# A fused adaLN transformer block: the last four quads in token halves, spaced modulation pieces, and three banks for VectorE's tiles

## The chip, the cores and the metric

The kernel runs on one core of a Trainium2 chip. The metric is device time in microseconds of one execution. Before the change the median of 3 runs is 764.55 us (762.23 to 765.07). The engines are TensorE (PE, matmuls into PSUM), VectorE (DVE), ScalarE (ACT), GpSimd (POOL) and SyncE (SP, which issues nearly all DMAs). PSUM has 8 banks of 512 fp32 columns.

## The reference

One block with adaptive layer norm: six modulation vectors come from `c`, attention with 32 heads of 16 columns follows, then a feed-forward of 1376 columns; S = 2048 tokens, D = 512, bf16 inputs.

```python
mod = (silu(c) @ w_mod).reshape(1, 6, 1, -1)
sa, ca, ga, sb, cb, gb = (mod[:, i] for i in range(6))
h = layernorm(x) * (1 + ca) + sa
x = x + ga * attention(h, wqkv, wo)         # softmax(q k^T / 4) v, 32 heads
h = layernorm(x) * (1 + cb) + sb
x = x + gb * (gelu(h @ w1 + b1) @ w2 + b2)
```

## The kernel before

**Work.** The tokens form four blocks b of 512. A quad is one block of queries with four heads, one in each 32-row strip of PE; there are 32 quads, in order of block. A quad has 16 key tiles for each of its four heads, so there are 32 x 64 = 2048 score tiles of 128 keys by 512 queries. A score tile is one matmul (`qk`, L819). Then it is exponentiated in one of two ways. ScalarE takes two or three PSUM banks at once with an exact exp into `PB` (L1254). VectorE takes one bank (`TB`, L1349): it makes the bits of a power of two as an int16, shifts the result twice (L1383), and PE adds the three approximations with the scaled values `VV`. The products with the values (L1028) add up in PSUM bank 7, the only one for this, so one quad's sum must be copied out (`emit_out`, L1304, into `o_sb`, a ring of two buffers) before the next may start.

**Normalizing a quad.** The softmax denominators lie in rows of `o_sb`. SP carries them through DRAM into `dall`, VectorE inverts them (L1319), SP carries them back, spread over rows, into `RB[par]` (L1324), and POOL multiplies (L1328) and adds the even and odd quads of a pair into `OT` (L1331). The last two quads are split instead into two halves of 256 tokens each (`LAST = NQ - 2`, `emit_half`): shuffle, reciprocal and product on VectorE (L1285 to L1289), with no trip through DRAM. Key tiles are paired there, so that a score tile again has 512 columns.

**Banks.** Exp groups of ScalarE use the zones (0, 1) and (3, 4); zone (0, 1) takes bank 2 as a third when it is free (`EXTRA`). VectorE's tiles use banks 6 and 5 (`D_BANKS`). All other matmuls, "sums" such as projections and feed-forward, take a free one of 2, 5 and 6 (`BG_BANKS`).

**Order.** The program writes every engine's instructions out by hand order at build time: a loop keeps a clock for each engine, and `step_pe`, `step_act`, `step_dve` and `run_alone` choose what that engine does next by planned durations. A step has `needs` (labels) and a `pos`: it may start when so many score tiles have been issued. `D_LOAD` and `D_ALONE` bound how much planned VectorE work may be waiting when another tile is given to VectorE. Fillers (L1092, L1095) are matmuls on zeros that PE does when too little has streamed in the last 3.4 us.

**Around attention.** `mod2_pieces` makes the second modulation's columns with 32 matmuls of one column (L496), in eight pieces. `tail_steps(b, base, sp)` holds, for blocks 0 to 2, the output projection, residual, norm and feed-forward, at positions spread by `SPREAD[b]`; its bias is added by VectorE (L604) and one GELU per block runs on ScalarE over 5632 columns (L614), which costs a table load there and another back. `last_steps` does the same for block 3 in two halves (`half(0)`, `half(1)`): the output projection's sum is added to `x1` (L673), `bn_stats` (L189) reads `x1`, POOL takes the root, then norm (L692), transposes (L699), up-projection (L708), GELU straight from PSUM on ScalarE (L712, only when no exps are left), down-projection (L720), residual and output (L727, L728).

Of the kernel before, what the change touches and what calls it, by code (L numbers as in the profile page):

```python
# [11 lines left out]
ALU = mybir.AluOpType  # L12
# [32 lines left out]
KEEP = 0.72  # L45
NQM = 5
# [3 lines left out]
D_BANKS = (6, 5)  # L50
BG_BANKS = (2, 5, 6)
BG_STRICT = False
D_LOAD = 2300.0
D_ALONE = 1400.0
# [16 lines left out]
SPREAD = (1.0, 1.0, 1.0)  # L71
# [16 lines left out]
def adaln_block(ctx: ExitStack, tc: tile.TileContext, A_x, A_wqkv, A_wo, B_x, B_w1, B_b1, B_w2, B_b2,  # L88
# [274 lines left out]
    LAST = NQ - 2  # L363
    quads += quads[LAST:]
    QN = NQ + 2
# [8 lines left out]
    class Step:  # L374
        def __init__(self, kind, eng, dur, fn, needs=(), label=None, pos=0, pieces=(), dt=FP32, alt=None, pdur=226.0,
                     mark=None):
            self.kind, self.eng, self.dur, self.fn = kind, eng, dur, fn
            self.needs, self.label, self.pos = tuple(needs), label, pos
            self.pieces, self.dt, self.alt, self.pdur = list(pieces), dt, alt, pdur
            self.bank, self.ready, self.done = None, None, 0  # L380
            self.only, self.gate, self.mode = False, None, "f" if dt is BF16 or label == "mod2" else "p"
# [123 lines left out]
    mm(mod2_pieces(), mod2_evac, 250.0, "mod2", [], rows_at, FP32, None, 260.0)  # L505
# [132 lines left out]
    def last_steps(base):  # L638
# [18 lines left out]
        op("SP", 0.0, begin, ("tb", b), [("te", b - 1)], base - 100)  # L657
        op("SP", 0.0, lambda: None, "spare", [], base - 60)

        def half(hf):  # L660
            tts = (2 * hf, 2 * hf + 1)
            cs = slice(256 * hf, 256 * hf + 256)
            at = base + 52 * hf

            def o_pieces(tt):
                def one(i, key, ch):
                    def f(ps):
                        mm4(ps, OT[key][:, tt * P:(tt + 1) * P], W_o[:, ch, :], i == 0, i == NC)
                    return f
                return [one(i, key, ch) for i, (key, ch) in enumerate(parts)]  # L670

            def o_evac(tt):
                return lambda ps, e: nc.vector.tensor_tensor(out=T["x1"][:, tt, :], in0=ps, in1=T["x1"][:, tt, :],  # L673
                                                             op=ALU.add)

            for tt in tts:
                x = mm(o_pieces(tt), o_evac(tt), 600.0, ("o", b, tt),
                       [("ot", b, ch) for ch in range(NC - 1)] + [("last", hf, 0), ("tb", b), ("wo", NC - 1)], at)
                x.gate = (NC, [("last", hf, 1)])
                op("DVE", 600.0, lambda tt=tt: ln_stats(T["x1"], T["st"], tt, tt), ("s2", b, tt), [("o", b, tt)])  # L680
# [8 lines left out]
            op("POOL", ROOT_L, root, ("r2", hf, b), [("a2", hf, b)])  # L689
            for i, tt in enumerate(tts):  # L690
# [3 lines left out]
                op("DVE", 325.0, norm, ("n2", hf, i), [("r2", hf, b), "spare"])  # L694
# [11 lines left out]
            for fc in range(NFC):  # L706
# [4 lines left out]
                def up(ps, e, fc=fc):  # L711
                    nc.scalar.activation(out=T["u"][:, fc, cs], in_=ps[:, 0:256], func=ACT.Gelu_apprx_tanh,  # L712
                                         bias=late["b1c"][:, fc:fc + 1], scale=1.0)
                x = mm([one(j) for j in range(NC)], up, 380.0, ("u3", hf, fc), [("h3", hf, j) for j in range(NC)],
                       at + 6, FP32, 380.0, 108.0)
                x.only, x.mode = True, "f"
# [14 lines left out]
            for tt in tts:  # L731
                x = mm(d_pieces(tt), d_evac(tt), 600.0, ("d", b, tt),
                       [("u3", hf, fc) for fc in range(NFC)] + [("w2", NFC - 1)], 2046 + hf, FP32, None,
                       216.0)
# [69 lines left out]
    def tok_of(qi):  # L804
        if qi < LAST:
            return slice(0, 512)
        hf = (qi - LAST) // 2
# [85 lines left out]
    def due_sum(t):  # L893
# [4 lines left out]
        for s in sums:  # L898
            if s.pos > scored[0]:
                return None  # L900
            if s.bank is None:
# [7 lines left out]
    def pe_burst(t, z):  # L909
        bs = list(ZONES[z]) if z is not None else []  # L910
        x = EXTRA[z] if z is not None else None
        if x is not None and free[x] <= t and not (busy_sum[0] is None and reserve(t)):
# [17 lines left out]
        if d_wanted(t):  # L930
            for r in d_rows(used):
# [3 lines left out]
                b_ = next((i for i in D_BANKS if free[i] <= t and i not in [x[0] for x in dp]), None)  # L935
# [102 lines left out]

    def pe_sum(t):
        s = busy_sum[0]  # L1040
        if s is None:
# [3 lines left out]
            if s.bank is None:  # L1045
                b_ = bg_bank(t)
                if b_ is None:
                    return False
                s.bank = b_
                free[b_] = INF  # L1050
            else:
# [8 lines left out]
        if s.gate and s.done == s.gate[0] and not has(s.gate[1], clk["PE"]):  # L1060
            sums.remove(s)
            held.append(s)
            busy_sum[0] = None
# [45 lines left out]
    def step_pe_work(t):  # L1109
# [32 lines left out]
        have = busy_sum[0] is not None or (due_sum(t) is not None and bg_bank(t) is not None)  # L1142
# [3 lines left out]
        if have:  # L1146
            s = busy_sum[0] or due_sum(t)
# [15 lines left out]
    def pool_ok(s, t):  # L1163
# [6 lines left out]
        if s.label[0] == "vv" or t > s.ready + POOL_WAIT:  # L1170
# [5 lines left out]
    def run_alone(e, t, maxpos=None):  # L1176
        n = 0
        for s in alone:
            if s.eng != e:
                continue  # L1180
            if s.pos <= scored[0] and has(s.needs, t):
                if e == "POOL" and not pool_ok(s, t):
# [3 lines left out]
                alone.remove(s)  # L1186
                made = s.fn()
                if e == "POOL" and made is not None:
# [9 lines left out]
                if e == "POOL" and s.label != "late" and s.label[0] not in ("r", "r2"):  # L1198
                    plock[0] = clk[e]
                if s.label is not None:  # L1200
# [22 lines left out]
    def take_evac(e, t):  # L1223
        for s in evacs:
            if s.only and (e == "DVE" or any(rowq) or filled):
                continue
            if s.ready + (0.0 if e == "DVE" else L_PA - L_PE) <= t and (e == "DVE" or s.alt is not None):
# [4 lines left out]
                free[s.bank] = v  # L1232
# [4 lines left out]
    def step_act(t):  # L1237
# [29 lines left out]
        if not warm and not any(rowq) and not filled:  # L1267
# [9 lines left out]
    warm = []  # L1277

    def emit_half(qi, t):
        hf, par = divmod(qi - LAST, 2)  # L1280
# [4 lines left out]
        nc.vector.tensor_copy(out=o[:, cs], in_=PS[:, 7, cs])  # L1285
        od_free[0] = t + 334.0 + L_DVE
        nc.vector.stream_shuffle(out=rs[:, cs], in_=o[:, cs], mask=[16 - par] * 32)
        nc.vector.reciprocal(out=rs[:, cs], in_=rs[:, cs])
        nc.vector.scalar_tensor_tensor(out=OT["last", par][:, cs], in0=o[:, cs], scalar=pmask[:, par:par + 1],  # L1289
                                       in1=rs[:, cs], op0=ALU.mult, op1=ALU.mult)  # L1290
        clk["DVE"] = t + 2950.0
# [279 lines left out]
```

## Time and profile before

| | us |
|---|---|
| median of 3 runs | 764.55 |
| the profiled execution | 765.63 |
| its span, first to last instruction | 763.9 |
| ScalarE: exps (L1254) busy | 679.3 |
| VectorE: tile fills (L1349) and shifts (L1383) busy | 368.3 and 221.9 |
| block 2's last output eviction (L626) starts | 723.1 |
| block 3's x is loaded (L652 issued) | 724.2 |
| last exp ends | 734.1 |
| first and last GELU of block 3 (L712) start | 738.2 and 751.7 |

All times of rows are from the span's start. The page lists busy time by engine and by line; the views by stretch, of waits and of the timeline cut the same execution in other ways. A row's mean is the duration of one instruction, and consecutive instructions of an engine overlap a little, so the distance between starts is shorter. The granted clock is the share of full speed that PE had.

### The profile page before, as it was taken

Reading aid. Unit: us, or ns where it says so; the run is one execution under the profiler, and the core shown is the slowest. Engines: PE = TensorE matmul, PEld = TensorE weight load, DVE = VectorE, ACT = ScalarE, POOL = GpSimd, SP = SyncE. Lnnn points to the kernel's source line nnn. Section 1 sums busy time; section 2 is a strip of 40 time slices with the busy share of each in tenths; the row PEclk is TensorE's granted clock in tenths of the full one; section 3 lists DMA queues with packets and bytes.
Section 4 is the critical chain, followed back from the end, with each engine's and each line's share of the span. In section 5 each row is a group of like instructions: output and inputs, shape, how many; then the busy total and the mean of one; then the engine's idle time right before and its main releaser. Section 6 shows DMA issues by size and latency. Waiting matters only on the chain.

```text
span 763.9 us, 20459 instructions
## 1 busy us (share of the span) xinstructions
PE 737.2 (97%) x8478; PEld 258.7 (34%) x8478; DVE 700.5 (92%) x1450; ACT 721.7 (94%) x671; POOL 108.9 (14%) x134
## 2 busy tenths in 40 slices
PE   3999999999999999999999999999999999999997
PEld 2433233233333333332333333332333332333454
DVE  6859999699999999988999999999899999999982
ACT  2889999899999999999999999999999999999982
POOL 3460010214232010100001110100101110100110
PEclk9999999799999999999999999999999999999999
DMA  8300000041010000000010000000000000000000
GB/s 274 112 2 11 10 6 6 9 151 16 10 37 9 10 4 8 9 16 24 15 38 3 15 4 10 9 17 12 22 18 30 9 10 9 9 10 23 21 28 31
DMA packets 27572, 20.43 MB, mean 27 GB/s; under 512 B 13801, under 2 KB 23386, under 8 KB 27474
## 3 DMA queue, kind: packets, MB, share of 16 engines
q1 hardware_dynamic: 26946, 19.07, 9.0%
q8 instruction: 68, 1.11, 0.6%
q14 instruction: 30, 0.25, 0.1%
q10 hardware_dynamic: 528, 0.00, 0.0%
HBM read 16.45 MB, written 2.61 MB: 25 GB/s over the span
## 4 chain that ended last, share of the span: by engine, by line
PE 57%; ACT 26%; DVE 9%; issue 5%; DMA 2%; SPq 1%; POOL 0%; ACTq 0%; DVEq 0%
ACT PB L1254 23%; PE PS L819 20%; PE PS L1028 18%; PE PS L406 12%; DVE TB L1349 4%; DVE TB L1383 2%; ACT uG L614 2%; PE PS L1092 2%; DMA xb<-in_A_x_dram 1%; PE PS L720 1%; PE PS L708 1%; PE PS L1095 1%; PE PS L213 1%; DVE st L189 1%; ACT L1254 0%
## 5 line engine op out<-in xcount | busy, mean ns | idle before, releaser
L1254 ACT ACTIVATE PB<-PS 128x1024 bf16<-128x1024 f32 x623 | 679.3, 1299 | 9.5 <-PE PS L819 7.7
L1349 DVE TENSOR_SCALAR TB<-PS 128x512 int16<-128x512 f32 x556 | 368.3, 682 | 22.1 <-PE PS L819 20.6
L819 PE MATMUL PS<-qm,kT 32*128 32x512 bf16 (+1 forms) x2176 | 301.9, 372 | 5.8 <-ACT PB L1254 2.8
L1028 PE MATMUL PS<-PB,VE 128*32 128x512 bf16 (+1 forms) x1589 | 252.0, 374 | 0.3 <-ACT PB L1254 0.3
L1383 DVE TENSOR_SCALAR TB<-TB 128x1024 int16<-128x1024 int16 x556 | 221.9, 421 | 5.3 <-PE PS L1028 0.5
L1028 PE MATMUL PS<-TB,VV 128*32 128x512 f16 (+1 forms) x1174 | 219.8, 374 | 0.3 <-DVE TB L1383 0.2
L819 PEld LDWEIGHTS <-kT 32*128 32x128 bf16 x2176 | 81.1, 91 | 244.5 <-issue 236.0
L1028 PE MATMUL PS<-TB,VE 128*32 128x512 f16 (+1 forms) x587 | 148.4, 375 | 1.2 <-DVE o_sb L1304 1.2
L1028 PEld LDWEIGHTS <-VE 128*32 128x32 bf16 x2176 | 69.0, 94 | 82.2 <-issue 72.1
L1028 PEld LDWEIGHTS <-VV 128*32 128x32 bf16 x1174 | 55.0, 95 | 43.7 <-issue 38.7
L1092 PE MATMUL PS<-W_q,zero 128*32 128x256 bf16 x360 | 66.7, 273 | 1.8 <-DVE TB L1349 1.4
L1328 POOL TENSOR_TENSOR OT<-o_sb,rb 128x512 bf16<-128x512 f32 x15 | 19.1, 1274 | 252.4 <-DVE TB L1383 140.7
L1328 POOL TENSOR_TENSOR o_sb<-o_sb,rb 128x512 f32<-128x512 f32 x15 | 19.1, 1270 | 247.4 <-DVE TB L1383 199.2
L406 PE MATMUL PS<-W,uG 128*32 128x512 bf16 x528 | 44.8, 383 | 0.0
L406 PE MATMUL PS<-h2T,W 128*32 128x512 bf16 x528 | 43.4, 384 | 0.2 <-DVE TB L1349 0.2
L1092 PEld LDWEIGHTS <-zero 128*32 128x32 bf16 x360 | 33.0, 96 | 23.2 <-issue 8.4
L1095 PE MATMUL PS<-W_q,zero 128*32 128x256 bf16 x163 | 34.4, 276 | 0.0
L604 DVE TENSOR_SCALAR uG<-PS,b1c 128x512 bf16<-128x512 f32 x33 | 24.6, 744 | 0.2
L406 PE MATMUL PS<-W_o,OT 128*32 128x512 bf16 x272 | 21.0, 383 | 0.6 <-DVE OT L1289 0.6
L1304 DVE COPY o_sb<-PS 128x512 f32<-128x512 f32 x30 | 20.4, 680 | 0.0
L1331 POOL TENSOR_TENSOR OT<-OT,o_sb 128x512 bf16<-128x512 bf16 x15 | 17.4, 1162 | 20.8 <-DVE TB L1383 11.7
L406 PE MATMUL PS<-hT,W_q 128*32 128x512 bf16 x240 | 20.0, 384 | 0.2 <-DVE TB L1349 0.2
(110 smaller groups left out, 401.6 us busy)
## 6 DMA issues: line engine op xcount, KB each, us to landing
rb<-d SPq DMA_DIRECT2D x120, 32.0 KB
W_m<-in_w_mod_dram SPq DMA_DIRECT2D x3, 1024.0 KB
xr<-in_A_x_dram SPq DMA_DIRECT2D x4, 512.0 KB
out_dram<-ob SPq DMA_DIRECT2D x16, 128.0 KB
xb<-in_A_x_dram SPq DMA_DIRECT2D x3, 512.0 KB
W<-in_B_w_dram SPq DMA_DIRECT2D x1, 1376.0 KB
W<-in_B_w_dram SPq DMA_DIRECT2D x1, 1280.0 KB
xb<-in_A_x_dram SPq DMA_DIRECT2D x4, 128.0 KB
```

The lines of the kernel that those rows point to most:

```text
L406: nc.tensor.matmul(out=ps[cols, :], lhsT=lhsT[:, cols], rhs=rhs, start=start, stop=stop)
L604: return lambda ps, e: nc.vector.tensor_scalar(out=T["u"][:, fc, :], in0=ps, scalar1=late["b1c"][:, fc:fc + 1], scalar2=None, op0=ALU.add)
L819: nc.tensor.matmul(out=bk(bank)[:, seg(qi, i)], lhsT=kT[32 * r:32 * r + 32, ch, kt[i] * P:(kt[i] + 1) * P], rhs=qm[(b, ch)][32 * r:32 * r ...
L1028: nc.tensor.matmul(out=PS[32 * r:32 * r + 32, 7, tok_of(qi)], lhsT=wt, rhs=src[:, seg(qi, i)], start=not started[qi][r], stop=todo[qi][r] ...
L1092: nc.tensor.matmul(out=PS[0:32, b_, 0:256], lhsT=zero, rhs=W_q[:, 0, 0:256], start=True, stop=True)
L1095: nc.tensor.matmul(out=PS[32 * o_:32 * o_ + 32, 7, c_:c_ + 256], lhsT=zero, rhs=W_q[:, 0, 0:256], start=False, stop=False)
L1254: nc.scalar.activation(out=PB[:, at:at + n, :], in_=PS[:, b0:b0 + n, :], func=ACT.Exp, bias=-KEXP * math.log(2.0), scale=math.log(2.0) / STEP)
L1304: made = nc.vector.tensor_copy(out=o, in_=bk(7))
L1328: return nc.gpsimd.tensor_tensor(out=o if par else ot, in0=o, in1=rb, op=ALU.mult)
L1331: return nc.gpsimd.tensor_tensor(out=ot, in0=ot, in1=o, op=ALU.add)
L1349: made = nc.vector.tensor_scalar(out=TB[:, u["a"]["s"], i:i + n, :], in0=PS[:, b0:b0 + n, :], scalar1=T_BIAS, scalar2=0.0, op0=ALU.add, op ...
L1383: made = nc.vector.tensor_scalar(out=TB[:, s, 0:n, :], in0=TB[:, a["s"], 0:n, :], scalar1=float(MJ[j] - MJ[j - 1]), scalar2=None, op0=ALU.add)
```

## The change

Four things change, with the planned costs that go with them.

- **Halves.** `HV = 4`: the last four quads, not two, run in token halves, in the order 28 to 31 for tokens 0 to 255 and then 28 to 31 for tokens 256 to 511. Quads 28 and 29 keep the normalization through DRAM and POOL, in halves; 30 and 31 use `emit_half`. The last half-quad of all skips its copy out of PSUM. The first half's projection, norm and up-projection come among the last exps: VectorE adds the bias, and one GELU per half runs when the exps are over (`gelu_raw`). The residual is now added on PE, with the identity times `x1` as the first piece of the sum; `bn_stats` reads PSUM, and `x1` is copied out of PSUM after the statistics. A down-projection of the last half starts before its last three GELUs.
- **Modulation.** After each of its eight pieces the step rests 1500 ns of planned time (`rest`), keeping its bank.
- **Banks.** VectorE's tiles use banks 5, 6 and 2; ScalarE's third bank is taken only if more than one of them is free (`X_FREE`). Both load bounds are lower.
- **Block 2's tail** is spread over 0.65 of the distance.

```diff
+HV = 4
+MOD_REST = 1500.0
-D_BANKS = (6, 5)
+D_BANKS = (5, 6, 2)
-D_LOAD = 2300.0
+D_LOAD = 1800.0
+X_FREE = 1
-D_ALONE = 1400.0
+D_ALONE = 900.0
-SPREAD = (1.0, 1.0, 1.0)
+SPREAD = (1.0, 1.0, 0.65)
...
-    LAST = NQ - 2
+    LAST = NQ - HV
     quads += quads[LAST:]
-    QN = NQ + 2
+    QN = NQ + HV
...
-    mm(mod2_pieces(), mod2_evac, 250.0, "mod2", [], rows_at, FP32, None, 260.0)
+    mm(mod2_pieces(), mod2_evac, 250.0, "mod2", [], rows_at, FP32, None, 300.0).rest = MOD_REST
...
-        op("SP", 0.0, begin, ("tb", b), [("te", b - 1)], base - 100)
-        op("SP", 0.0, lambda: None, "spare", [], base - 60)
+        op("SP", 0.0, begin, ("tb", b), [("te", b - 1)], 1880)
+        op("SP", 0.0, lambda: None, "spare", [], 1920)
...
-            at = base + 52 * hf
+            early = HV == 4 and hf == 0
+            raw = []
+            at = base + 52 * hf if HV == 2 else (1950, 2032)[hf]
...
-                return [one(i, key, ch) for i, (key, ch) in enumerate(parts)]
+                return [lambda ps: mm4(ps, ident, T["x1"][:, tt, :], True, False)] + [
+                    one(i, key, ch) for i, (key, ch) in enumerate(parts)]
...
+                    nc.vector.bn_stats(out=T["st"][:, tt, :], in_=ps)
...
+                    nc.vector.tensor_copy(out=T["x1"][:, tt, :], in_=banks[tt])
...
+                    if e == "dve":
+                        raw.append(fc)
+                        nc.vector.tensor_scalar(out=T["u"][:, fc, cs], in0=ps[:, 0:256],
+                                                scalar1=late["b1c"][:, fc:fc + 1], scalar2=None, op0=ALU.add)
+                    else:
+                        nc.scalar.activation(out=T["u"][:, fc, cs], in_=ps[:, 0:256], func=ACT.Gelu_apprx_tanh,
+                                             bias=late["b1c"][:, fc:fc + 1], scale=1.0)
-                x.only, x.mode = True, "f"
+                x.only, x.mode = "late" if early else True, "f"
+
+            def gelu_raw():
...
+                    u = T["u"][:, 0:len(raw), cs]
+                    nc.scalar.activation(out=u, in_=u, func=ACT.Gelu_apprx_tanh)
...
+                       ([("g3", hf)] if early else []) + [("u3", hf, fc) for fc in range(NFC - 3)] + [("w2", NFC - 1)],
+                       2046 + hf, FP32, None, 216.0)
+                x.gate = (NFC - 3, [("u3", hf, fc) for fc in range(NFC - 3, NFC)])
...
-        if x is not None and free[x] <= t and not (busy_sum[0] is None and reserve(t)):
+        if (x is not None and free[x] <= t and not (busy_sum[0] is None and reserve(t))
+                and sum(1 for i in D_BANKS if free[i] <= t) > X_FREE):
             bs.append(x)
...
+        if s.rest and s.done < len(s.pieces):
+            s.ready = clk["PE"] + s.rest
             busy_sum[0] = None
             return True
...
+            if s.label[0] == "d" and s.pos >= 2046 and ("n2", 1, 1) not in rdy:
+                continue
...
     def emit_half(qi, t):
+        src = PS[:, 7, cs] if qi == QN - 1 else o[:, cs]
+        if qi < QN - 1:
+            nc.vector.tensor_copy(out=src, in_=PS[:, 7, cs])
...
     def emit_out(qi, t):
+        hf = None if qi < LAST else (qi - LAST) // HV
+        if hf is not None and (qi - LAST) % HV >= HV - 2:
             return emit_half(qi, t)
...
+        cs = tok_of(qi)
+        n = cs.stop - cs.start
...
+        made = nc.vector.tensor_copy(out=o[:, cs], in_=PS[:, 7, cs])
...
+                nc.sync.dma_start(out=rb[rows, cs], in_=d2[r:r + 1, :].to_broadcast([16, n]))
...
+            return nc.gpsimd.tensor_tensor(out=(o if par else ot)[:, cs], in0=o[:, cs], in1=rb[:, cs], op=ALU.mult)
```

Also new: while scores are over, a down-projection may be set aside for a step of an earlier position (`paused`); POOL's products no longer wait for cover in the last three half-quads; the separate warm-up activation of GELU (L1269) is dropped.

More of the change, by code (lines that the diff above doesn't have):

```diff
@@ L900, in due_sum @@
                 return None
+            if s.rest and s.bank is not None and s.done < len(s.pieces) and t >= s.ready:
+                return s
             if s.bank is None:
@@ L934, in pe_burst @@
                     continue
-                b_ = next((i for i in D_BANKS if free[i] <= t and i not in [x[0] for x in dp]), None)
+                b_ = next((i for i in D_BANKS if free[i] <= t and i not in bs[:len(take)] + [x[0] for x in dp]), None)
                 if b_ is None:
@@ L1199, in run_alone @@
                     plock[0] = clk[e]
+                if s.frees is not None:
+                    free[s.frees.bank] = clk[e] + L_DVE
                 if s.label is not None:
```

136 lines of the change are left out of this document (86 added, 50 removed).

## The prediction

> **What bounds the kernel now.** I read the page's busy shares first, then busy time by stretches of 16 to 20 us, then the exp groups by shape, the waits, and the last 30 us as a timeline.
>
> ```profile
> span 763.9 us, 20459 instructions
> PE 737.2 (97%) x8478; PEld 258.7 (34%) x8478; DVE 700.5 (92%) x1450; ACT 721.7 (94%) x671; POOL 108.9 (14%) x134
> ```
>
> PE's 97% is the weakest of these: it is pipelined, and its row holds 523 filler matmuls (L1092, L1095), work that nothing needs. ScalarE and VectorE bind: they share the 2048 score tiles, and from 160 to 734 us both are busy in nearly every stretch. So I price the middle in tiles. Exp groups by shape:
>
> ```profile
> L1254 ACT ACTIVATE PB<-PS 128x1024 bf16<-128x1024 f32 x365 | 387.6, 1136 | 1.7 <-PE PS L819 1.2 <-PE PS L1028 0.2
> L1254 ACT ACTIVATE PB<-PS 128x1536 bf16<-128x1536 f32 x240 | 373.4, 1556 | 5.6 <-PE PS L819 4.3 <-PE PS L1028 1.2
> ```
>
> From one exp's start to the next the trace has 0.904 us after two banks and 1.331 after three: 0.452 and 0.444 us a tile. VectorE's tile costs 0.60 (a fill, L1349, start to next start) and 0.33 (its share of the shifts, L1383): 0.93. Together 2.25 + 1.08 = 3.33 tiles per us, so 1 us of VectorE work is worth 0.32 us of span and 1 us of ScalarE work 0.68. Two places fall short of that rate. The first, by stretches (PE, weight loads, DVE, ACT, POOL; granted clock after them):
>
> ```profile
> 136.00:152.00 16.00, 15.75 (x149) 4.35 (x148) 9.10 (x19) 13.34 (x13) 4.04 (x4) 0.68 0.00 1
> 152.00:168.00 16.00, 15.95 (x188) 5.03 (x185) 15.28 (x32) 16.00 (x17) 3.75 (x6) 1.00 0.31 95
> ```
>
> Here the granted clock falls to half, from about 137 to 147 us, 2 us after the 32 one-column matmuls of the second modulation begin (L496, 135.0 to 141.4). The second is the end (timeline; start, length):
>
> ```profile
> 734.11 1.28 ACT L1269 ACT_TABLE_LOAD   x1
> 736.38 1.75 DVE L1288 RECIPROCAL rb<-rb 128x256 f32<-128x256 f32 x1
> 739.24 1.29 DVE L673 TENSOR_TENSOR xr<-PS,xr 128x512 bf16<-128x512 f32 x2 [0.58 <-PE PS L406]
> 740.44 1.28 DVE L189 BATCH_NORM_STATS2 st<-xr 128x6 f32<-128x512 bf16 x2
> 743.08 0.73 DVE L692 TENSOR_SCALAR TB<-xr,mv,rs 128x512 bf16<-128x512 bf16 x2 [1.14 <-POOL rs L200]
> 744.37 2.54 PE L720 MATMUL PS<-W,uG 128*128 128x512 bf16 x11
> 746.74 4.97 PE L708 MATMUL PS<-h2T,W 128*128 128x256 bf16 x44
> 751.54 2.54 PE L720 MATMUL PS<-W,uG 128*128 128x512 bf16 x11
> 754.11 4.92 PE L720 MATMUL PS<-W,uG 128*128 128x512 bf16 x22
> 759.07 0.69 DVE L727 TENSOR_TENSOR ob<-PS,xr 128x512 bf16<-128x512 f32 x1 [1.63 <-PE PS L720]
> ```
>
> The last exp ends at 734.11 and 29.8 us follow. The first half's two down-projections stand in this chain, one ahead of the second half's up-projection and one behind it.
>
> **The sum.** It is made against the profiled run: 765.63 us, span 763.9. That run is 1.08 above the median of 764.55; I scale at the end.
>
> 1. *Spaced modulation.* In the slow stretch ScalarE lost 16.00 - 13.34 = 2.66 us (6.0 tiles), VectorE 15.28 - 9.10 = 6.18 us (6.7 tiles); 12.7 / 3.33 = 3.8 us. Eight pieces a planned 1.5 us apart put under 0.4 us of them in any 1.8 us, where before five stood in 2.4 us. They hold their PSUM bank about 14 us, not 6.6, so I take **-3.2** (bounds 0, the clock falls anyway, and -3.8). The weights waiting on it are loaded near 165 us and first used by L604 at 262: hidden.
> The Trainium skill ("TensorE: Matmul & The Clock Gate", "What's actually happening") ties half rate to an idle window of some 3.4 us; PE shows none here (15.75 of 16.00 busy), so by its letter spacing changes nothing, and the sum would be 3.2 higher. The row, a drop right behind the one-column matmuls, decides for me: they occupy PE's row without filling the array. The reading stays as a rival.
>
> 2. *The end.* The last half-quad skips its copy (L1285 0.42): -0.4. The residual add goes into the PSUM sum, so the statistics follow L406 directly: x1's 1.2 us (two at 0.60) leave the path; the two copies that replace them take 1.25 beside POOL's root, whose gap is 1.14: -1.1. The norm starts near 741.55, h2T is ready at 743.75 rather than 745.27. Then 4.97 (up) and 4.92 (two downs) follow without the 2.54 between: PE ends at 753.7 plus what is left of the first half's downs. These wait for the GELU: table load 1.28, and half of L614's 4.90 for half the columns, so 734.1 + 1.3 + 2.5 = 737.9; 5.0 of downs and 1.4 of the other half's pieces end at 744.4, 0.65 late. PE 754.3 against 759.03: **-4.7** (bounds: -5.4 nothing late; -2.2 one down-projection still stands in the chain).
> The Trainium skill ("ScalarE: Activation LUTs", "What ACT_TABLE_LOAD costs") adds a drain and gives 2.66 us a switch. The trace has the next activation at 735.40, 1.29 after the load began; by the page this item would be 1.4 us smaller.
>
> 3. *What moves in front of the last exp.* On VectorE: 11 bias evictions of 256 columns, not shown before; between half of L604's 0.66 pitch (0.33) and L1285's 0.46, taken 0.40: 4.4. Two norms 0.74, four h2T evictions 1.5, two more small reciprocals (L1319 0.24) and four 0.35 copies for two of 0.60: 0.7. Sum 7.3 us, times 0.32: **+2.3** (bounds 1.9 and 2.8). On PE: up 4.97, transposes 0.9, identity pieces 0.9, shorter matmuls for two more quads about 1.4: 8 us, covered by fillers (64 from 640 to 734 us, at 0.113 a 256-column matmul by L708: 7.2): **+0.7** (bounds 0 and +4, half of it uncovered). SP gets 14 more issues (0.3 to 0.5 us each), into a queue with idle time between all of them; POOL's products are halved, not added to.
>
> 4. *Three banks.* VectorE still waited for scores:
>
> ```profile
> DVE TB L1349 <- PE PS L819: 11.0, 21, 0.9
> ```
>
> This is 160 to 640 us; 1.4 more follow. A third bank can return all 12.4 x 0.32 = 4.0. The order 5, 6 also lets one fill read both banks: before, all 556 are single. A copy of 256 columns lasts 0.416 and of 512 0.680, so 512 columns cost 0.53 of the 0.60 pitch and each joined pair saves 0.07; 278 pairs would be 19 us, 6.2 of span. Against it: bank 2 is ScalarE's third. If all 240 triples became pairs, 720 x 8.3 ns = 6 us x 0.68 = +4.1. I take a third of the waits (-1.3), 30% of the pairs (-1.9) and a fifth of the triples (+0.8): **-2.4** (bounds -10 and +4.1).
>
> The spread 0.65 of block 2's tail moves the same instructions earlier, where 640 to 680 has the fillers: 0; it lets x for block 3 land before 724.2, where its load is issued now.
>
> Sum: -3.2 - 4.7 + 2.3 + 0.7 - 2.4 = -7.3: 758.3 against 765.63, or **757.2** against the median.
>
> **Rivals.**
> - *The clock falls anyway* (chance 0.12): +3.2, 760.4. For: no PE idle in the row. Against: its timing.
> - *Triples are lost and the third bank returns nothing* (0.14): +2.4 + 4.1, 763.7. For: ScalarE has no idle time to give. Against: a triple saves only 8 ns a tile.
> - *PE binds the last 80 us* (0.08): fillers there are 11 from 680 on, so item 3's PE work shows in full: +4, 761.2.
> - *VectorE stalls on the ring of two o_sb buffers* (0.10, the slower side). Half-quad n+2 takes the buffer and the reciprocal rows of n, free only when POOL has multiplied n. The last copies start at 719.27, 727.08 and 735.45: two half-quads are 16.2 us. For quad 29:
>
> ```profile
> 695.40 0.68 DVE L1304 COPY o_sb<-PS 128x512 f32<-128x512 f32 x1
> 707.49 1.27 POOL L1328 TENSOR_TENSOR o_sb<-o_sb,rb 128x512 f32<-128x512 f32 x1 [16.70 <-DMA rb<-d]
> ```
>
> That is 12.1 us to the product; other quads take up to 18.8. With 0.6 to 1.3 for the halved products the ring is free after 12.7 to 20.1. Past 16.2 VectorE stands at the copy, behind it the exp fills, and bank 7 stays shut, so PE stops in order and ScalarE runs dry: full price. At a mean 3 us for four reuses +12: 769. Against: most trips are near 15, and before the change no such wait is in the waits.
>
> **How the numbers follow.** My forecast has 0.56, with its own range 753.5 to 760.5 (item 4 is most of it). A measurement can tell about 0.5%, 3.8 us: faster is under 760.7, slower over 768.4. Faster: 0.55 + 0.08 + 0.03 + 0.03 = 0.69. Slower: 0.07 of the stall, 0.03 of several bounds at once: 0.10. Same: 0.21. The range runs from 751.5 (half of item 4's lower bound) to 765, above the lost triples; about 0.06 and 0.12 lie outside.
>
> **What would show it.** Item 1: the granted clock stays at 1.00 from 130 to 160 us. Item 2: from the last exp to the end 25 us rather than 29.8, one GELU of about 2.5 us behind the table load, and no L720 matmul between the up-projection and the second half's downs. Item 3: the bias evictions among the exps, and VectorE's tiles about 8 fewer there. Item 4: fills of 128x1024, shorter waits of L1349, and no fewer than 190 triples. I would be wrong if VectorE waits for POOL at a copy or shuffle in the last 80 us, if triples fall under 100, or if the clock drops in a new place.

## The result, and the profile after

The changed kernel takes **766.18 us** (763.47 to 768.97, 20 runs), the kernel before, on the same chip, 764.18 (762.08 to 765.45, 20 runs): ratio 1.0029, interval 1.0018 to 1.004. So it is 0.3% slower, little but clear of the noise. The forecast was 757.2, in a range of 751.5 to 765.0. The profiled execution took 766.15, its span 763.6 (before: 765.63 and 763.9). Page of after, busy shares:

```profile
span 763.6 us, 21448 instructions
PE 735.1 (96%) x8890; PEld 262.3 (34%) x8890; DVE 707.1 (93%) x1426; ACT 720.7 (94%) x742; POOL 110.5 (14%) x137
```

VectorE works 6.6 us more and ScalarE has 71 more instructions in the same span. Groups by shape, ScalarE's exps and VectorE's fills:

```profile
L1326 ACT ACTIVATE PB<-PS 128x1024 bf16<-128x1024 f32 x625 | 595.3, 1162 | 11.4 <-PE PS L859 10.2 <-PE PS L1071 1.0
L1326 ACT ACTIVATE PB<-PS 128x1536 bf16<-128x1536 f32 x78 | 124.4, 1595 | 1.7 <-PE PS L859 1.7
...
L1431 DVE TENSOR_SCALAR TB<-PS 128x512 int16<-128x512 f32 x458 | 306.6, 683 | 18.2 <-PE PS L859 16.7
L1431 DVE TENSOR_SCALAR TB<-PS 128x1024 int16<-128x1024 f32 x52 | 63.3, 1217 | 1.0 <-PE PS L859 0.7
```

Triples fell from 246 (240 of them in the stretch from 45 to 735 us that the prediction shows) to 78, so nearly all exps are pairs now; 52 fills read two banks at once. VectorE's wait for scores from 184 to 640 us (us in total, times, longest) is less than half of the 11.0 before (the same in this stretch):

```profile
DVE TB L1431 <- PE PS L859: 5.0, 17, 0.7
```

**Where the time went.** Busy time by five stretches (length, PE, weight loads, DVE, ACT, POOL, granted clock, DMA share, GB/s). Before:

```profile
136.00:164.00 28.00, 27.70 (x287) 8.04 (x286) 20.48 (x41) 25.34 (x25) 7.80 (x9) 0.82 0.04 8
164.00:184.00 20.00, 19.57 (x208) 6.67 (x207) 19.40 (x40) 19.28 (x18) 5.11 (x5) 1.00 0.50 150
184.00:640.00 456.00, 449.95 (x4988) 149.22 (x4984) 439.02 (x907) 453.92 (x408) 55.57 (x49) 1.00 0.06 15
640.00:700.00 60.00, 59.89 (x708) 20.33 (x704) 57.12 (x118) 59.94 (x53) 3.71 (x3) 1.00 0.05 9
700.00:725.00 25.00, 25.00 (x477) 11.03 (x472) 24.57 (x50) 24.97 (x27) 2.43 (x2) 1.00 0.09 24
```

After:

```profile
136.00:164.00 28.00, 27.23 (x305) 9.07 (x297) 19.70 (x37) 28.00 (x32) 8.43 (x8) 1.00 0.04 8
164.00:184.00 20.00, 17.71 (x180) 5.91 (x175) 17.40 (x35) 16.84 (x17) 2.67 (x5) 0.91 0.52 150
184.00:640.00 456.00, 451.35 (x5125) 149.97 (x5118) 445.97 (x890) 455.54 (x457) 57.39 (x49) 1.00 0.06 15
640.00:700.00 60.00, 58.87 (x1078) 26.32 (x1076) 58.65 (x119) 59.27 (x60) 5.84 (x6) 1.00 0.06 15
700.00:725.00 25.00, 22.18 (x387) 9.11 (x384) 21.22 (x48) 21.24 (x23) 1.62 (x3) 0.93 0.13 32
```

Busy time doesn't say what was got done. For that I counted, in the trace, the banks of scores whose exp or fill had started by the end of each stretch. All 2048 are found in every trace, so nothing is missing from the account; at 3.33 tiles per us it converts to time. The count starts at the first instruction of an engine, 0.25 us after the span's start:

| tiles started | before | after | difference | us of span |
|---|---|---|---|---|
| to 136 us | 309 | 311 | +2 | -0.6 |
| 136 to 164 | 73 | 73 | 0 | 0 |
| 164 to 184 | 61 | 53 | -8 | +2.4 |
| 184 to 640 | 1346 | 1353 | +7 | -2.1 |
| 640 to 700 | 168 | 163 | -5 | +1.5 |
| 700 to 725 | 72 | 62 | -10 | +3.0 |

An exp takes two or three tiles at once, so a row is good to some three tiles, about 1 us: with the edges at the span's own start, as in the views, the differences are +2, +2, -9, +7, -6 and -12. Together 14 tiles behind, 4.2 us; the last exp indeed ends 4.7 us later, at 738.76 instead of 734.09. Then the end wins 4.9 us back, and the spans are nearly equal. Two of these rows, 164 to 184 and 700 to 725, are stops that the forecast didn't have.

**First stop**, timeline of after:

```profile
167.15 0.68 DVE L1383 COPY o_sb<-PS 128x512 f32<-128x512 f32 x1
...
168.73 4.10 SPq L541 DMA_DIRECT2D b_bf<-in_B_b_dram  x1
...
173.28 0.25 SPq L545 DMA_DIRECT2D W<-in_B_b_dram  x1
...
173.65 0.51 SPq L1388 DMA_DIRECT2D d<-o_sb  x1
...
177.17 0.25 DVE L1399 RECIPROCAL rp<-dall 128x16 f32<-128x16 f32 x1 [2.01 <-DMA dall<-d]
...
177.75 0.38 PE L1071 MATMUL PS<-TB,VV 128*32 128x512 f16 x1 [1.96 <-DVE TB L1465]
```

Quad 5's denominators are in `o_sb` at 167.83, but SP's queue is busy with the late loads, 4.10 us of them one bias vector, and issues their DMA only at 173.65. VectorE's in-order stream then stands at the reciprocal for 2.01 us; the shifts are behind it, PE waits for a shift, and the clock falls to 0.79 from 176 to 184. Before, the copy started 2.05 us later and the DMA 0.54 us earlier (173.11), and the wait was short:

```profile
176.58 0.25 DVE L1319 RECIPROCAL rp<-dall 128x16 f32<-128x16 f32 x1 [0.49 <-DMA dall<-d]
```

**Second stop**, timeline of after:

```profile
700.25 0.68 DVE L630 TENSOR_TENSOR ob<-PS,xr 128x512 bf16<-128x512 f32 x1
...
701.35 1.73 SPq L656 DMA_DIRECT2D xr<-in_A_x_dram  x1
...
706.52 0.40 PE L410 MATMUL PS<-xr,ident 128*32 128x512 bf16 x4 [2.60 <-DMA xr<-in_A_x_dram]
...
707.28 1.02 ACT L1326 ACTIVATE PB<-PS 128x1024 bf16<-128x1024 f32 x1 [2.56 <-PE PS L859]
707.32 0.69 DVE L1431 TENSOR_SCALAR TB<-PS 128x512 int16<-128x512 f32 x1 [2.38 <-PE PS L859]
```

Block 3's `x` uses block 2's buffer, so its load is issued after block 2's last output. It takes 5.2 us from issue to PE's first use; the plan reckons 2.5. Before, VectorE read `x` 6 us after the issue (730.21), 4 us ahead of the last exp's end, and nothing waited. Now the identity times `x` is the *first* piece of the projection's sum on PE, which runs in order: both other engines go without scores behind it.

**The end**, timeline of after:

```profile
738.78 1.28 ACT L751 ACT_TABLE_LOAD   x1
...
740.07 1.91 ACT L751 ACTIVATE uG<-uG 128x2048 bf16<-128x2048 bf16 x1
...
741.89 1.19 ACT L739 ACTIVATE uG<-PS,b1c 128x256 bf16<-128x256 f32 x3
...
743.37 1.30 DVE L684 BATCH_NORM_STATS2 st<-PS 128x6 f32<-128x512 f32 x2 [1.02 <-PE PS L410]
743.39 4.06 PE L759 MATMUL PS<-W,uG 128*128 128x512 bf16 x18
...
746.55 0.74 DVE L714 TENSOR_SCALAR TB<-xr,mv,rs 128x512 bf16<-128x512 bf16 x2 [0.57 <-POOL rs L203]
...
748.92 4.97 PE L730 MATMUL PS<-h2T,W 128*128 128x256 bf16 x44
...
753.91 4.92 PE L759 MATMUL PS<-W,uG 128*128 128x512 bf16 x22
```

From the last exp to the end are 24.85 us (before 29.8). The GELU covers 2048 columns: 8 of the first half's 11 pieces had been made before the last exp. The first half's down-projections fill the time of statistics and norm, and none stands between up-projection and the second half's downs.

### The profile page after: what moved, and what is told of

It reads as the page before. It is cut to its first block, busy times and chain, and to the rows that moved or that the text cites. A ratio compares the mean times of both kernels' runs of the same rounds, so it can differ in the third digit from the quotient of the medians.

```text
span 763.6 us, 21448 instructions
## 1 busy us (share of the span) xinstructions
PE 735.1 (96%) x8890; PEld 262.3 (34%) x8890; DVE 707.1 (93%) x1426; ACT 720.7 (94%) x742; POOL 110.5 (14%) x137
## 5 line engine op out<-in xcount | busy, mean ns | idle before, releaser
L1326 ACT ACTIVATE PB<-PS 128x1024 bf16<-128x1024 f32 (+1 forms) x705 | 681.3, 1209 | 13.1 <-PE PS L859 11.9
L1431 DVE TENSOR_SCALAR TB<-PS 128x512 int16<-128x512 f32 (+1 forms) x510 | 369.6, 737 | 19.2 <-PE PS L859 17.4
L859 PE MATMUL PS<-qm,kT 32*128 32x512 bf16 (+1 forms) x2304 | 293.2, 359 | 6.6 <-ACT PB L1326 3.1
L1465 DVE TENSOR_SCALAR TB<-TB 128x1024 int16<-128x1024 int16 (+1 forms) x564 | 221.9, 419 | 4.5
L1152 PE MATMUL PS<-W_q,zero 128*32 128x256 bf16 x462 | 90.3, 273 | 1.4 <-DVE TB L1431 1.0
L1408 POOL TENSOR_TENSOR o_sb<-o_sb,rb 128x512 f32<-128x512 f32 (+1 forms) x16 | 19.3, 1204 | 249.9 <-DVE TB L1465 179.5
L1152 PEld LDWEIGHTS <-zero 128*32 128x32 bf16 x462 | 42.9, 96 | 29.3 <-issue 7.8
L1408 POOL TENSOR_TENSOR OT<-o_sb,rb 128x512 bf16<-128x512 f32 (+1 forms) x16 | 19.3, 1205 | 226.3 <-DVE TB L1465 204.7
L1155 PE MATMUL PS<-W_q,zero 128*32 128x256 bf16 x105 | 23.5, 277 | 0.0
L1411 POOL TENSOR_TENSOR OT<-OT,o_sb 128x512 bf16<-128x512 bf16 (+1 forms) x16 | 17.7, 1103 | 34.9 <-DVE TB L1465 31.9
L1383 DVE COPY o_sb<-PS 128x512 f32<-128x512 f32 (+1 forms) x32 | 20.7, 646 | 0.1
```

Of the source, the lines that this page charges most:

```text
L859: nc.tensor.matmul(out=bk(bank)[:, seg(qi, i)], lhsT=kT[32 * r:32 * r + 32, ch, kt[i] * P:(kt[i] + 1) * P], rhs=qm[(b, ch)][32 * r:32 * r ...
L1152: nc.tensor.matmul(out=PS[0:32, b_, 0:256], lhsT=zero, rhs=W_q[:, 0, 0:256], start=True, stop=True)
L1155: nc.tensor.matmul(out=PS[32 * o_:32 * o_ + 32, 7, c_:c_ + 256], lhsT=zero, rhs=W_q[:, 0, 0:256], start=False, stop=False)
L1326: nc.scalar.activation(out=PB[:, at:at + n, :], in_=PS[:, b0:b0 + n, :], func=ACT.Exp, bias=-KEXP * math.log(2.0), scale=math.log(2.0) / STEP)
L1383: made = nc.vector.tensor_copy(out=o[:, cs], in_=PS[:, 7, cs])
L1408: return nc.gpsimd.tensor_tensor(out=(o if par else ot)[:, cs], in0=o[:, cs], in1=rb[:, cs], op=ALU.mult)
```

## The experiments

The theories: **(A)** the four mechanisms work as forecast, and the loss is the two stops plus the bank that the spaced modulation holds; **(B)** the rivals of the prediction, or the banks, are the loss. Each version was timed beside the kernel before. A table of what was measured comes first; "184 to 640" is the count of tiles in that stretch.

| version | median us (range, runs) | before in the same call | ratio, interval | 184 to 640 |
|---|---|---|---|---|
| x_split | 764.04 (762.84 to 765.57, 12) | 763.63 | 1.0011 (0.9999 to 1.0023) | 1355 |
| no_rest | 761.18 (759.37 to 764.61, 12) | 763.63 | 0.997 (0.9956 to 0.9984) | 1355 |
| two_banks | 766.76 (766.44 to 766.98, 6) | 763.63 | 1.0049 (1.0032 to 1.0065) | 1331 |
| b1_early | 763.36 (761.22 to 765.21, 12) | 763.63 | 1.0002 (0.9988 to 1.0015) | 1355 |
| no_rest_x | 758.49 (758.14 to 759.31, 6) | 764.08 | 0.9936 (0.9916 to 0.9956) | 1353 |
| no_rest_x_2b | 765.59 (762.89 to 766.6, 12) | 764.08 | 1.0021 (1.0006 to 1.0037) | 1337 |
| before_3b | 763.3 (762.46 to 765.87, 12) | 764.08 | 1.0002 (0.9988 to 1.0017) | 1351 |
| before_rest | 764.82 (764.18 to 765.18, 12) | 764.08 | 1.0015 (1.0003 to 1.0027) | 1351 |
| all_three | 758.17 (757.77 to 759.11, 6) | 763.98 | 0.9936 (0.9918 to 0.9954) | 1355 |
| two_banks_b | 769.26 (768.28 to 771.6, 6) | 763.98 | 1.0084 (1.0064 to 1.0104) | 1335 |
| two_banks_c | 769.55 (768.82 to 772.91, 6) | 763.98 | 1.0083 (1.0064 to 1.0102) | 1323 |
| short_rest | 765.49 (762.69 to 767.43, 12) | 763.98 | 1.0018 (1.0002 to 1.0033) | 1354 |

**x_split**: `x` for block 3 in two loads, the first when two of block 2's outputs are out; the plan reckons 6.5 us.

```diff
-            nc.sync.dma_start(out=T["x1"], in_=x_tok[b])
+                nc.sync.dma_start(out=T["x1"][:, 2 * h:2 * h + 2, :], in_=x_tok[b][:, 2 * h:2 * h + 2, :])
...
+        op("SP", 0.0, load_x(0), ("tb", b, 0), [("d", b - 1, 0), ("d", b - 1, 1)], 1700)
+        op("SP", 0.0, load_x(1), ("tb", b, 1), [("te", b - 1)], 1700)
```

> The changed kernel with one thing different: block 3's x is loaded in two DMAs, the first half's as soon as block 2's first two outputs are evicted, and the plan reckons 6.5 us for a load and not 2.5. Theory (PE stall on x): in the changed kernel PE stands 2.6 us at L410 until xr lands at 706.5, then runs to 711 at half clock; ScalarE loses 3.8 us and VectorE 3.8 us of 702 to 712, 12.6 tiles, 3.8 us of span. So 762.4 us here, clock 1.00 from 700 to 715, no wait of PE on a DMA there, and the first half's up-projection done before the last exp. Rival (the stall is slack that another engine would have lost anyway): 766, the last exp where it was.

764.04; by the two ratios, 1.0011 and 1.0029, 1.4 us less than the changed kernel, where 3.8 had been expected. In the stretch view of x_split the last row is whole again, with 72 tiles where the changed kernel has 62 (and before 72):

```profile
700.00:725.00 25.00, 24.77 (x428) 11.06 (x416) 24.64 (x56) 24.69 (x28) 1.67 (x3) 1.00 0.09 21
```

The last exp ends at 734.21, 4.5 us sooner, but the end after it takes 27.8 us instead of 24.85:

```profile
735.52 0.84 ACT L759 ACTIVATE uG<-uG 128x768 bf16<-128x768 bf16 x1
```

Only 3 of the first half's 11 pieces stand in front of the last exp here (the GELU covers 768 columns), so the other eight follow it. The expectation had all of the up-projection done by then. So part of what the stop cost in the middle had been returned at the end, and its price is 1.4 us here (2.6 between no_rest and no_rest_x below, by their ratios) rather than 3.0. The first stop is still there (51 tiles from 164 to 184).

**no_rest**: the changed kernel without spacing.

```diff
-    mm(mod2_pieces(), mod2_evac, 250.0, "mod2", [], rows_at, FP32, None, 300.0).rest = MOD_REST
+    mm(mod2_pieces(), mod2_evac, 250.0, "mod2", [], rows_at, FP32, None, 260.0)
```

> The changed kernel with the second modulation's eight pieces back to back, as before the change. Theory (spacing gives back what it saves): the clock falls to half for some 10 us near 140 again (+3.8), but the step holds its bank 7 us and not 29, which returns the 8.3 us that VectorE stood idle from 136 to 164 (-2.7), so about +1, 767; a little less if the stop at 176 to 184 moves away with it (-2.6, 764.6). Rival A (the spacing pays in full, as predicted): 769 to 770. Rival B (the drop was not due to these matmuls): clock 1.00 near 140 without spacing, 763.5.

761.18: taking the spacing *out* gains 4.5 us by the ratios (0.997 and 1.0029), against the sign of item 1 and below all that had been expected; some 0.7 of it lies outside the span (see the last bullet of the next section). In this profiled execution the clock did fall, as before the change (no_rest, stretches of 4 us):

```profile
140.00:144.00 4.00, 3.96 (x28) 0.73 (x31) 2.74 (x7) 3.13 (x4) 1.19 (x1) 0.50 0.00 0
144.00:148.00 4.00, 4.00 (x41) 0.93 (x34) 2.94 (x6) 2.78 (x4) 1.03 (x1) 0.66 0.01 2
```

Yet 71 tiles start from 136 to 164, only two fewer than with spacing, and 60 follow by 184, seven more: the first stop is gone. Without the spacing the late loads begin 2.6 us sooner (161.25, with it 163.86), so quad 5's DMA waits for SP until 171.40, not 173.65, and the reciprocal finds its rows in time (174.88, no wait; before the change 176.58 and 0.49 us). Half of the executions of this version keep the clock: of the 12, six have a mean clock of at least 0.998, and the profiled one, at 0.990, is the longest (764.61). The second stop is still there (PE waits 1.63 us for `x`).

**two_banks**, **b1_early**: the changed kernel with VectorE's tiles back in two banks (and the planner's bounds of before), and with the feed-forward bias's small loads (SP's L541 among them) at the kernel's start, behind the second modulation's weights. The edit of two_banks:

```diff
-D_BANKS = (5, 6, 2)
+D_BANKS = (6, 5)
-D_LOAD = 1800.0
+D_LOAD = 2300.0
-X_FREE = 1
+X_FREE = -1
-D_ALONE = 900.0
+D_ALONE = 1400.0
```

The edit of b1_early:

```diff
     W_m2 = load_mod(2, nc.sync)
+    b1_bf = const.tile([P, NFC], BF16, name="b1_bf")
+    nc.gpsimd.memset(b1_bf, BIG)
+    nc.sync.dma_start(out=b1_bf[:, 0:NFC - 1], in_=B_b1[0:(NFC - 1) * P].rearrange("(j p) -> p j", p=P))
...
-        b1_bf = lw.tile([P, NFC], BF16, name="b1_bf")
```

> The changed kernel with banks 6 and 5 for VectorE's tiles, bank 2 free for ScalarE's third as before, and the two load bounds as before. Theory (triples are lost and little comes back): 246 triples and 623 exps instead of 78 and 705, so ScalarE's exps take 82 x 0.05 = 4.1 us less (-2.8 of span); the 52 joined fills are gone (+1.2); VectorE's waits for scores about as many; 764.6. Rival (the third bank pays for itself): 768, with VectorE waiting over 20 us on L859.

> The changed kernel with the two small loads of the bias b1 (one issue of 4.1 us on SP's queue at 168.7) moved from the late loads to the start of the kernel. Theory (SP's queue): in the changed kernel quad 5's copy is done at 167.5, but its DMA stands behind that issue until 173.65; VectorE then waits 2.0 us for dall, PE 2.0 us for VectorE, and the clock falls from 178 to 182: ScalarE loses 3.1 us and VectorE 1.7 from 176 to 184, 8.8 tiles, 2.6 us. So 763.5 here, with quad 5's first DMA within 1 us of its copy and clock 1.00 from 160 to 200. Rival (the weights' traffic on the DMA engines delays dall, not the queue): the wait stays, 766.

two_banks: 766.76, between the 764.6 of the theory and the 768 of the rival, and no better with 215 triples, so lost triples are not the loss. The time hides two things that cancel: neither stop is in its trace (60 tiles from 164 to 184, 73 from 700 to 725), but the middle starts 22 tiles fewer, 1331, and ScalarE stands 3.4 us near 686.

b1_early: 763.36, by the ratios 2.1 us better, the expected time, but in the profiled execution, the longest of the 12, only part of the first stop goes (ScalarE busy 5.90 of 8 us from 176 to 184, 4.91 in the changed kernel; clock 0.79 in both). SP's queue of b1_early:

```profile
165.71 4.09 SPq L542 DMA_DIRECT2D W<-in_B_w_dram  x1
...
170.24 0.51 SPq L1388 DMA_DIRECT2D d<-o_sb  x1
174.51 0.37 SPq L1390 DMA_DIRECT2D dall<-d  x1
```

Without the bias vector, a weight load holds the queue for 4.09 us, and quad 5's DMA is issued 3.4 us sooner than in the changed kernel (170.24, not 173.65). But the next leg follows only 4.27 us later, where it took 1.85: the DMA engines are full then (share 1.06 from 168 to 172). So the rows show two delays, the queue of the theory and, as the rival had it, the weights' traffic; what each costs was not separated.

**no_rest_x** and **no_rest_x_2b**: the edits of x_split and of no_rest together; the second has two_banks' edit as well.

> The changed kernel with the modulation's pieces back to back and x of block 3 loaded in two parts. Theory (two separate costs): without spacing 761.18, with x in two parts 764.04, the changed kernel 766.18; if the two places cost independently, 766.2 - 5.0 - 2.1 = 759.1, no wait of PE on a DMA near 700, and in runs where the clock holds near 140, 757. Rival (both only move the same slack, one of them is enough): 761.

> The same with banks 6 and 5 for VectorE's tiles, bank 2 free as ScalarE's third and the load bounds as before the change. It tells what the three banks are worth once nothing holds a bank for 29 us. Theory (they are worth little: joined fills and shorter waits against lost triples; with spacing, two banks were 0.6 us slower): 759 to 760. Rival A (the forecast of -2.4 was right): 761.5. Rival B (lost triples are the larger part, -2.8): 757.

no_rest_x: **758.49**, within 1.3 us of the forecast and 0.6% faster than the kernel before. It has the clock that item 1 was to bring without the spacing: five of its six executions are at 0.999 or above. Its stretches:

```profile
136.00:164.00 28.00, 27.15 (x333) 8.80 (x325) 25.41 (x52) 26.19 (x29) 7.79 (x9) 1.00 0.18 54
164.00:184.00 20.00, 18.94 (x195) 6.43 (x194) 18.94 (x38) 19.38 (x18) 5.29 (x5) 1.00 0.31 86
184.00:640.00 456.00, 449.13 (x5098) 147.28 (x5102) 446.98 (x894) 455.82 (x457) 55.12 (x48) 1.00 0.06 15
```

VectorE does 25.41 us of work from 136 to 164 where spacing left it 19.70; 77 tiles instead of 73. no_rest_x_2b: 765.59, 7.1 more and outside all three expectations. Part of that is one stop of 4.35 us of ScalarE near 660 us, where PE ran the tail's matmuls first; so the price of the banks stayed open.

**before_3b** and **before_rest**: one part alone, in the kernel before: three banks with their bounds and rule, or the spacing. The constants of before_3b, and the line of before_rest:

```diff
-D_BANKS = (6, 5)
+D_BANKS = (5, 6, 2)
-D_LOAD = 2300.0
+D_LOAD = 1800.0
+X_FREE = 1
-D_ALONE = 1400.0
+D_ALONE = 900.0
```

```diff
-    mm(mod2_pieces(), mod2_evac, 250.0, "mod2", [], rows_at, FP32, None, 260.0)
+    mm(mod2_pieces(), mod2_evac, 250.0, "mod2", [], rows_at, FP32, None, 300.0).rest = 1500.0
```

> The kernel before with only the three banks, their rule for the triple and the two load bounds. Rival A (the forecast): 763.6 - 2.4 = 761.2. Theory (worth little): 763 to 764, some 50 joined fills, under 100 triples. Rival B (triples): 766.

> The kernel before with only the spaced pieces. In 10 of its 29 runs of the last comparison the kernel before has a mean clock of 0.998 or 1.000 and spans of 759.8 to 760.6; in the others 0.992 to 0.996 and 761.5 to 763.6. So the drop near 140 does not come in every execution, and at most 1.6 us of the median is to be had. Theory (a held bank costs more than the clock): the step holds one of three banks for some 29 us, VectorE stands idle 8 us or more of it (-2.7 of span at least): 765 to 766, all runs near clock 0.999. Rival (the forecast, item 1): 760.4. Rival (both equal out): 763.6.

before_rest: the clock is at least 0.998 in all 12 executions, where before it falls in two thirds of them, and still 764.82, 0.7 *more*. Part of the reason is in its row:

```profile
136.00:164.00 28.00, 27.45 (x298) 9.83 (x295) 16.78 (x35) 28.00 (x29) 8.00 (x9) 1.00 0.14 46
```

VectorE has 16.78 of 28 us of work, less than the 20.48 with the clock at half, and the tiles started there are about as many (74, before 73). The end after the last exp also takes 31.4 us instead of 29.8. before_3b: 763.3, no measurable gain, though the middle goes as forecast (1351 tiles against 1346): its end after the last exp takes 31.7 us. Its pieces are back to back, and yet 10 of its 12 executions have a clock of at least 0.998, where the kernel before has that in 26 of 75. So spacing holds the clock, but is not the only thing that does.

**all_three**: no_rest_x with the small loads at the start as in b1_early.

> The changed kernel without spacing, block 3's x in two parts, and b1's small loads at the start of the kernel. In the version without the last edit the small loads hold the DMA-issuing queue for 5.03 us (163.8 to 168.8) and from 160 to 176 us VectorE is busy 13.05 of 16 us, ScalarE 14.48. Theory (the queue keeps quad 5's reciprocal rows waiting there, the rest is another cause): about half of that is regained, 0.7 us; 757.8 (756.8 to 758.8). Rival (the stretch is short of work because of bulk loads and the start of the row groups, not because of that queue): no change, 758.5 and the same busy times. Second rival (loads at the start delay the first quads): 759.5.

758.17, the best version. The first stop is gone here too (62 tiles from 164 to 184, 60 in no_rest_x):

```profile
164.00:184.00 20.00, 19.88 (x204) 6.97 (x203) 19.43 (x39) 20.00 (x19) 6.20 (x5) 1.00 0.27 81
```

The times alone can't tell it from no_rest_x; the row shows the theory's half (from 160 to 176 VectorE 13.62 and ScalarE 15.02 of 16 us).

**two_banks_b**, **two_banks_c**: two more courses of the plan with two banks, each with one of the two bounds of before. In no_rest_x, for two_banks_b (two_banks_c keeps `D_LOAD` and changes `D_ALONE` to 1400 instead):

```diff
-D_BANKS = (5, 6, 2)
+D_BANKS = (6, 5)
-D_LOAD = 1800.0
+D_LOAD = 2300.0
-X_FREE = 1
+X_FREE = -1
```

> No spacing, x in two parts, VectorE's tiles in two banks with VectorE's load bound of the kernel before (2300) but the lone-tile bound of the changed one (900): another course of the plan with two banks. The first such version took 765.59, 7.1 more than with three, and 4.4 us of that were one stop of ScalarE near 660 us (worth about 3.6 us of span with VectorE's share). Theory (the banks themselves are worth some 3 us, the rest was that stop): 761.5 to 763 if no such stop is in the trace, VectorE busy about 655 us from 45 to 736; 764 to 766.5 if there is one. Rival (the banks are worth nothing, the stop all): 758 to 760 without a stop. Second rival (the banks are worth all 7 us): 764.5 or more without a stop.

> As two_banks_b with the bounds the other way round (VectorE's load bound 1800 of the changed kernel, lone-tile bound 1400 of the one before). The same numbers: with banks worth some 3 us, 761.5 to 763 without a stop and up to 766.5 with one; 758 to 760 if the banks are worth nothing; 764.5 or more without a stop if they are worth 7.

769.26 and 769.55, neither with a stop of ScalarE over 1.5 us from 640 to 725 (two_banks_c has one of 4.3 us before). The expectation of 3 us was wrong, and so was "the stop was all": going from three banks, with their rule and bounds, to two costs the unspaced halves kernel 7 to 11 us (about 1 us of it outside the span in no_rest_x_2b and two_banks_c), some of it by stops (two_banks_b has the first stop, 53 tiles from 164 to 184), most of it in the middle. From 184 to 640, eight versions with three banks start 1351 to 1355 tiles, whatever else they have, and six with two start 1323 to 1351. The row of two_banks_c:

```profile
184.00:640.00 456.00, 450.41 (x4962) 146.64 (x4958) 435.10 (x891) 448.28 (x400) 55.98 (x48) 1.00 0.06 14
```

VectorE does 11.7 us less work there than in all_three, and ScalarE 7.6 (two_banks_c's profiled execution is its longest, 772.91). So with the third bank the middle hardly depends on the plan's course in these versions; the kernel before had one of the better courses with two. Two banks with both lower bounds were not run, so the bank itself is not parted from its bounds. Why the halves' plans with two banks come out below it in a stretch where no half runs yet is open.

**short_rest**: x_split with a spacing of 0.5 us instead of 1.5.

```diff
-MOD_REST = 1500.0
+MOD_REST = 500.0
```

> Spacing 0.5 us instead of 1.5, x in two parts. The spaced version took 764.04 and the unspaced 758.49. Theory (the price of the spacing is the PSUM bank it holds, 29 us with pieces 4.2 us apart): pieces come 2 to 3 us apart, the bank is held 14 to 20 us, and the price falls by a third to a half: 760.5 to 762.2, with the clock at 1.00 from 130 to 160 us. Rival (the price is the late course of the loads behind the modulation, the stop at 176 to 184 us, in or out): 758.5 to 759.5 if that stop is gone and 763 to 764.5 if it is there.

765.49. The held bank costs less, as expected (VectorE 23.09 of 28 us from 136 to 164, between 19.53 and 25.41), but the first stop is there and longer:

```profile
176.00:184.00 8.00, 6.47 (x49) 1.42 (x48) 6.85 (x13) 4.24 (x4) 1.73 (x2) 0.69 0.09 19
```

46 tiles from 164 to 184, 16 fewer than in all_three, 4.8 us, and the time lies above both expectations. The larger price here seems to be not the bank but how the steps behind the modulation meet quad 5: its copy now starts at 166.68 while SP is busy until 171.9, and VectorE waits 2.20 us for the reciprocal's rows. Another part is a stop of 2.43 us of ScalarE until 165.44, while PE works off projections and products with the values; no run parts the two.

## Why the prediction was wrong, step by step

- **Item 1 (-3.2) failed, in three places.** "They hold their PSUM bank about 14 us": the pieces came 4.2 us apart and the bank was held 29 us, 133.9 to 163.4, so VectorE lost by it about what the clock returned: 73 tiles before and after (71 and 73 with the views' edges), where 12.7 were to come back. And the base was one execution. Over the 75 timed executions of before, 26 have a clock of at least 0.998 and a median span of 760.2 us, 49 a lower one and 762.5: the fall is worth 2.3 us in two of three executions. The profiled one, at 763.9, was above them all. Its surplus of 1.08 may well have been the same fall, counted twice when it was taken off at the end: 763.9 - 3.2 - 1.1 is 759.6, below the 760.2 of the executions that keep the clock. That is not shown. The sentence "the weights waiting on it are loaded near 165 us: hidden" costed at nothing the 2.4 us of the first stop: the weights have time, but quad 5's DMA, behind them on the queue and beside them on the DMA engines, has not.
- **Item 2 (-4.7) held, in part by luck**: 24.85 us after the last exp against the 25 foretold. The norm starts 7.8 us after it (forecast 7.45), the GELU takes 1.91 us rather than 2.5 (8 pieces, not 11), and the second half's PE chain ends 20.1 us after it (forecast 20.2). But the 8 pieces got in front of the last exp while the exps were late: in x_split, no_rest_x and all_three, where the second stop is gone, 3 did, and the end takes 26.7 to 27.8 us; in two_banks_b, whose last exp ends as late as 742.8, all 11 did, and the end takes 23.7. The GELU follows the table load's start by 1.29 us. The Trainium skill ("ScalarE: Activation LUTs", "What ACT_TABLE_LOAD costs") gives a load and a drain, 2.66 us, for every switch; by that, an estimate, the GELU would start 1.4 us later, and no run here shows it.
- **Item 3 (+3.0) held in size, but what it left out decided.** From 640 to 700 five tiles are missing, 1.5 us; in no_rest_x and all_three three to five by 725 (0.9 to 1.5 us), and the end there takes 26.7 to 26.9 us instead of 24.85, so about 3 in all. Of 11 bias evictions VectorE got 8. The prediction noted that the early tail lets `x` land sooner, and costed that at nothing; that PE now needs `x` *first* in an in-order stream was not asked. It cost 10 tiles, 3.0 us, of which loading it in two parts brought back 1.4 us in the time, and 2.6 in the unspaced kernel.
- **Item 4 (-2.4) held as a sum in the middle**: +7 tiles, 2.1 us; alone, in before_3b, it brought no gain in the time. Its terms were off: the waits gave back half, not a third; 52 pairs were joined, not 83, each saving the 0.07 us foretold (start to start 1.135 against 2 x 0.60); and 78 triples stayed where "no fewer than 190" was the mark, without the loss that was to show. Of the prediction's own signs of being wrong two came: fewer than 100 triples, and the clock falling in new places (0.79 from 176 to 184, 0.93 from 700 to 725).
- **The rivals.** "The clock falls anyway" did not happen. "Triples are lost and the bank returns nothing" was right in its first half only. PE didn't bind the last 80 us: 47 fillers still stand from 640 to 734 us (63 before). VectorE waited for POOL at no copy; the late thing in its stream was a DMA, in a place that no rival named.
- **What is left.** Time less span is 2.17 to 2.81 us in 20 executions of the changed kernel and 1.73 to 1.90 in 75 of the kernel before; no_rest, no_rest_x and all_three are back at 1.73 to 1.91, and so are two_banks and short_rest, which keep a spacing, while b1_early has 2.42 to 2.72. That 0.7 us lies outside what the trace shows; its cause is open.

So by tiles 9.0 us of error are: item 1 3.2, first stop 2.4, second stop 3.0, outside the span 0.7, and the 1.1 taken off at the end; the other terms give 1.4 back. This is an account, not a measurement of each term. What the runs measure is what taking a cause out brings, by the ratios: 4.5 us without the spacing (item 1's loss, the first stop and the 0.7 together), 1.4 with `x` in two parts, 7.1 with both.

## What to carry to other kernels

When an operand moves from a late engine to the first piece of a sum on an in-order engine, ask when its load lands, and when that load can be issued at all: the buffer's last reader sets that. Spacing or delaying a step costs the resource that it holds meanwhile and shifts everything behind it on its queue, so price both before the gain. And count work done by a time (tiles, here) rather than busy time: an account by stretch told in one table what the engines' shares could not. It says where work is missing; what a fix returns must be run.

## What the runs showed of the hardware

- The granted clock can fall to half while PE has work without a gap: 0.50 from 140 to 144 us in no_rest with PE busy 3.96 of 4.00. The same program falls in some executions and not in others: of the 75 of the kernel before, 49 have a mean clock below 0.998. The Trainium skill ("TensorE: Matmul & The Clock Gate", "What's actually happening") describes a free-running activity window, so that the moment of the first warm-up depends on where in it the first matmul lands. The scatter here would fit that, but no run shows it, and the idle window that the page asks for is not in the rows.
- A load of ten single values per partition holds SP's queue long: 4.10 us for the bias vector at 168.73, longer than the longest weight load ahead of it (2.54). Weight loads vary too: the longest one takes 2.21 us in all_three and 4.09 in b1_early. 512 KB of `x` in one DMA need 5.2 us from issue to use.
- A fill over two banks (1.217 us busy) saves 5% of two single ones, start to start.
